# Decay rows of the first four units spread by 128-row matmuls, with more filling matmuls, in a scan and two MLP layers on one core

## Chip, core and metric

The kernel runs on one core of one Trainium2 chip. The metric is the device time of one execution in microseconds (us), taken as the median of several runs. The engines are PE (TensorE), DVE (VectorE), ACT (ScalarE), POOL (GpSimd) and SP (SyncE, which issues the DMAs).

## What is computed

A chunked linear scan with a decay feeds two MLP layers, all in float32:

```python
# scan: batch 4, 8 heads, 768 tokens, head_dim 32, state 16
L = exp(cum[i] - cum[j]) * (i >= j)          # products of the decays a
M = (C @ B.T) * L
y = M @ x + (C @ state) * exp(cum)
state = decay_full * state + sum_j B_j x_j decay_from_j
# x = y as (3072, 256)
h = x @ w_in                                  # 256 x 2048
g = where(h > 0, h, exp(min(h, 0)) - 1)
x = g @ w_out                                 # 2048 x 256
out = ((x @ w_a) * (x @ w_b)) @ w_out2        # 1536 wide
```

## The kernel before

The scan is cut into 24 units of 128 tokens of one batch with all 8 heads (`unit`, u = 0 to 23). Tokens go through the MLP in six tiles of 512 columns (phase A, `pair`), and afterwards through the gated layer (phase B, `group`). Tile 0 needs units 0 to 3, tile 1 needs units 4 to 7, and so on. The weights of w_in and w_out for tile 0 come in as raw words and are decoded on ACT, DVE and POOL (`weight`, lines 405 to 423).

**One unit.** The decay rows of its 8 heads have to stand in all 128 partitions. Units from 4 on load them by a broadcasting DMA from `a_seg` (line 522). Units 0 to 3 take them from `a32`, the first 32 rows of the decays (4 units of 8 heads), with float32 matmuls (`spread`, line 536): the weights are column r of the identity `delta`, repeated 128 times, the moving operand is `a32`, and 128 copies of row r land in PSUM. There are two groups of four heads. Then come a DVE scan against `delta` (line 560), the score matmuls of 16 rows (`cbm`, line 598, two groups of four heads, which for units 0 to 7 sit in different row ranges of `sm`), a DVE mask (line 601), the output matmuls into `ybank` (`ym`, lines 629, 633 and 637), and ACT copies of the state and of x out of `ybank` (lines 651 and 669 for units 0 to 3).

**Filling matmuls.** `warm` (line 299) multiplies a zero tile `zt` with itself in bfloat16 into the last quarter of `ybank`. Nobody reads the result. 44 of them open the program, and the planner may put more where it expects PE to be idle.

**The order.** `Plan` is a list scheduler. Each step has engines with a cost, predecessors and a due time. `emit` repeatedly takes the ready step that could start first (ties by due time) and writes it on its engine, so each engine's order is fixed before the program runs. Ahead of a PE step that starts before `FILL_TO` with over 0.2 us of expected idle time, `emit` writes fillers, their number being the idle time divided by a constant (line 140). Steps carry a `weight` for the planner's own model of PE's speed (`pe_clock`). The due times of tile 0 start at `T1`, and those of most later steps hang on it. Fillers write into `ybank`, so the first filler of a row waits for the readers of the unit before it.

Of the kernel before, what the change touches and what calls it, by code (L numbers as in the profile page):

```python
# [9 lines left out]
F32 = mybir.dt.float32  # L10
# [7 lines left out]
P = 128  # L18
NB, NH, S, D, N = 4, 8, 768, 32, 16
# [19 lines left out]
PUT_DVE = [1, 0, 1, 0, 1, 0, 1, 0, 0, 0, 0, 0, 0, 0, 0, 0, 0]  # L39
REST_DVE = [1, 1, 1, 1, 0, 1, 0, 1, 1, 0, 1, 0, 1, 0, 1, 0, 1]  # L40

T1, PAIR1, PAIR, GROUP = 22.0, 8.0, 6.2, 14.96
LEAD, GAP = 30.0, 11.0
NFILL, FILL_TO = 44, 30.0


class Buf:
# [10 lines left out]
class Plan:  # L58
# [11 lines left out]
    def add(self, engines, fn, *after, due, port=False, pad=0.0, weight=1.0, nb=0.7):  # L70
        flat = []
        for a in after:
            flat += a if isinstance(a, list) else [a]
        self.steps.append((engines, fn, [a for a in flat if a is not None], due, port, pad, weight, nb))
        return len(self.steps) - 1
# [14 lines left out]
    def emit(self, go=True):  # L90
        n = len(self.steps)
        self.work = {}
        left, then, ends = [0] * n, [[] for _ in range(n)], [None] * n
        for i, s in enumerate(self.steps):
            for a in set(s[2]):
                left[i] += 1
                then[a].append(i)
        free = dict.fromkeys(("PE", "ACT", "DVE", "POOL", "SP"), 0.7)
        port, dma, done = 0.0, 0.0, 0
        self.log = []  # L100
        ready = []

        def enter(i):
            engines, fn, after, due, prt, pad, weight, nb = self.steps[i]
            opts = []
            for e, c in engines.items():
                at = nb
                for a in after:
                    end, ea = ends[a]
                    end += (self.SYNC[ea] if ea != e else self.SAME[e]) + (pad if ea != e else 0.0)  # L110
                    if end > at:
                        at = end
                opts.append((e, c, at))
            ready.append((due, i, opts, prt))

        for i in range(n):
            if not left[i]:
                enter(i)
        while ready:
            best = None  # L120
            for k, (due, i, opts, prt) in enumerate(ready):
                end = None
                for e1, c1, at in opts:
                    s1 = free[e1] if free[e1] > at else at
                    if e1 == "POOL" or (e1 == "DVE" and prt):
                        if port > s1:
                            s1 = port
                    if e1 == "SP":
                        e, start, c = e1, s1, c1
                        break  # L130
                    if end is None or s1 + c1 < end:
                        e, start, end, c = e1, s1, s1 + c1, c1
                key = (math.floor(start / self.WIN), due, i)
                if best is None or key < best[0]:
                    best = key, k, i, e, start, c
            _, k, i, e, start, c = best
            due, _, _, prt = ready.pop(k)
            if e == "PE":
                if self.fill and go and start < FILL_TO and start - free["PE"] > 0.2:
                    m = int((start - free["PE"]) / 0.06)  # L140
                    self.fill(m)
                    self.pe_clock(free["PE"], 0.055 * m, 1.0)
                end = self.pe_clock(start, c, self.steps[i][6])
                free[e] = end
            elif e == "SP":
                end = start
                for kb in c:
                    dma = max(dma, end + 1.75) + kb / 250.0
                    end += 0.45
                free[e], end = end, dma + 0.6  # L150
            else:
                end = start + c
                free[e] = end
                if e == "POOL" or prt:
                    port = end
            if go:
                self.steps[i][1](e)
            self.log.append((i, e, start, end))
            ends[i] = end, e
            done += 1  # L160
            for t in then[i]:
                left[t] -= 1
                if not left[t]:
                    enter(t)
        assert done == n
        return max(free.values())
# [3 lines left out]
def kernel(  # L170
# [14 lines left out]
    nc = tc.nc  # L185
# [4 lines left out]
    def tl(shape, dt, name):  # L190
        return sb.tile(shape, dt, name=name, tag=name)


    delta = tl([P, 4, P], F32, "delta")
# [70 lines left out]
    def flat4(bf):  # L265
        return bf.ap.rearrange("p h i -> p (h i)") if len(bf.ap.shape) == 3 else bf.ap
# [5 lines left out]
    add = plan.add  # L272
# [4 lines left out]
    def nxt(ring, name):  # L277
        k = cnt.get(name, 0)
        cnt[name] = k + 1
        return ring[k % len(ring)]  # L280
# [42 lines left out]
                                     op0=ALU.mult, op1=ALU.add)  # L323


    a32 = tl([4 * NH, P], F32, "a32")

    def decay_0(e):
        nc.vector.tensor_scalar(a32, a32, 1.0, 1e-6, op0=ALU.min, op1=ALU.max)
        nc.vector.memset(a32[:, 0:1], 0.0)  # L330

    d0 = -40.0
    i_a0 = add({"SP": [16]}, lambda e: nc.sync.dma_start(a32, al[0:4 * NH, :]), due=d0 - 1)
    i_dec0 = add({"DVE": 0.3}, decay_0, i_a0, due=d0 - 1)
    i_z = add({"POOL": 0.2}, zeros, due=d0)
    i_warm = add({"PE": 0.055 * NFILL}, lambda e: warm(NFILL), i_z, due=d0)
# [2 lines left out]
    i_ones = add({"POOL": 1.6}, ones, due=d0)  # L339
# [146 lines left out]
    def unit(u, due):  # L486

        c, b = divmod(u, NB)
        s, r = divmod(u, NG)
# [7 lines left out]
        pd = 0.6 if u >= UPT else 0.0  # L497
# [26 lines left out]
        if n:  # L524
            i_ab = add({"SP": [512]}, ld_a, ab.take(), i_seg, due=due - ld, nb=due - ld - 10)
        else:

            sp, cb_ = ([accb[0], accb[1]], [nxt(cb1, "cb1") for _ in range(2)]) if u < 2 else (
                [nxt(rest3, "r3") for _ in range(2)], [nxt(rest3, "r3") for _ in range(2)])
            i_ab = []  # L530
            ab_old = ab.take()
            for g in range(2):
                def spread(e, g=g):
                    for h in range(4):
                        r = u * NH + 4 * g + h
                        nc.tensor.matmul(flat4(sp[g])[:, h * P:(h + 1) * P], delta[0:4 * NH, 0, r:r + 1].to_broadcast([4 * NH, P]),
                                         a32, start=True, stop=True)

                i_ab.append(add({"PE": 1.08}, spread, sp[g].take(), i_dec0, i_ones, ab_old, due=due - 1))
                sp[g].users.append(i_ab[-1])  # L540
        if s:
            i_sm = add({"SP": [512]}, ld_sm, sm.take(), i_parts[s], due=due - ld, nb=due - ld - 10)
            smu = sm
        else:
            if u % 2 == 0:
                first_sm[0] = sb_.take()
            i_sm = add({"SP": [64, 64]}, ld0, first_sm[0], due=due - ld, nb=due - ld - 10)
# [37 lines left out]
        for g in range(2):  # L585
            h4 = slice(4 * g, 4 * g + 4)

            cb = cb_[g] if n == 0 else cbb

            def cbm(e, g=g, cbank=cb.ap if len(cb.ap.shape) == 3 else cb.ap.rearrange("p (h i) -> p h i", h=4)):  # L590
                for h in range(4):
                    if s == 0:
                        q = slice(h * P, (h + 1) * P)
                        t = sm32[row + 32 * g:row + 32 * g + N]
                    else:
                        q = slice((4 * g + h) * P, (4 * g + h + 1) * P)
                        t = sm.ap
                    nc.tensor.matmul(cbank[:, h, :], t[:, 0, q], t[:, 1, q], start=True, stop=True)  # L598

            def mask(e, h4=h4, cbank=cb.ap if len(cb.ap.shape) == 3 else cb.ap.rearrange("p (h i) -> p h i", h=4)):  # L600
                nc.vector.tensor_mul(lt[:, h4], cbank, lt[:, h4])

            i_cb = add({"PE": 0.28 if s else 1.0}, cbm, cb.take(), i_sm, due=due, pad=pd)
            smu.users.append(i_cb)
            i_k = add({"DVE": 0.685}, mask, i_cb, i_scan[g], i_le, due=due)
            cb.users += [i_cb, i_k]
            i_msk.append(i_k)
# [749 lines left out]
```

## Time and profile before

| | before |
|---|---|
| median of 3 runs | 637.32 us (636.58 to 639.22) |
| the profiled execution | 636.4 us |
| its span in the trace | 634.7 us |
| PE busy | 625.9 us, 99% of the span, 3540 matmuls |
| DVE, ACT, POOL busy | 61%, 59%, 54% |

The engines' busy time is an average over stages. A PE that is busy without a gap may still run at half of its speed, so its granted clock is read beside its busy time. The chain of waits is followed back from the last instruction; where it names PE, PE was what the end waited for.

### The profile page before, as it was taken

The numbers are of one execution on the slowest core, as the hardware profiler recorded it, in microseconds if no ns is written. First come the engines' busy times: TensorE is split into PE (matmuls) and PEld (weight loads), VectorE is DVE, ScalarE is ACT, GpSimd is POOL, SyncE is SP. The second block draws the span as 40 slices with busy tenths as digits, with TensorE's granted clock in tenths as the row PEclk, the third lists the DMA queues.
The fourth block names the chain that finished last, engine by engine and source line by source line (L and its number), as shares of the span: only waits on it lengthen the run. The fifth ranks groups of instructions, "written<-read, shape, count | busy, mean of one in ns | idle before, by whom it ended". The sixth has DMA issues, their size and how long they took to land.

```text
span 634.7 us, 9280 instructions
## 1 busy us (share of the span) xinstructions
PE 625.9 (99%) x3540; PEld 490.2 (77%) x3540; DVE 386.8 (61%) x517; ACT 375.5 (59%) x536; POOL 340.3 (54%) x260
## 2 busy tenths in 40 slices
PE   9999999999999999999999999999999999999996
PEld 8875545778877788777888888888888888888885
DVE  6558886888755976987654565545633447333333
ACT  2237667657776786666677755456554456654553
POOL 2034347354765566556448287567755566555552
PEclk8579999999999999999999999999999999999999
DMA  7926643666759755620000000000100000100001
GB/s 243 322 86 220 229 142 99 226 239 195 228 161 311 237 173 158 208 84 0 2 1 0 2 0 1 0 2 0 67 2 0 1 1 1 67 1 0 1 0 67
DMA packets 33308, 59.89 MB, mean 94 GB/s; under 512 B 2736, under 2 KB 13808, under 8 KB 33264
## 3 DMA queue, kind: packets, MB, share of 16 engines
q1 hardware_dynamic: 33264, 59.30, 28.5%
q8 instruction: 28, 0.46, 0.3%
q14 instruction: 16, 0.13, 0.1%
HBM read 47.56 MB, written 11.73 MB: 93 GB/s over the span
## 4 chain that ended last, share of the span: by engine, by line
PE 90%; DMA 3%; DVE 2%; POOL 2%; issue 1%; ACT 1%; DVEq 0%; ACTq 0%; SPq 0%; POOLq 0%
PE up L1036 5%; PE up L1033 5%; PE up L1032 5%; PE up L695 5%; PE up L704 5%; PE up L705 5%; PE up L707 5%; PE acc L720 5%; PE acc L716 4%; PE acc L717 4%; PE acc L695 4%; PE acc L1104 4%; PE acc L1105 4%; PE acc L1106 4%; PE cbank L598 3%; PE cbank L1104 3%
## 5 line engine op out<-in xcount | busy, mean ns | idle before, releaser
L1133 DVE TENSOR_TENSOR x<-x 128x512 f32<-128x512 f32 x36 | 29.9, 835 | 82.0 <-POOL x L1177 81.6
L1139 POOL TENSOR_TENSOR gl<-x,gh 128x512 fp32r<-128x512 f32 x35 | 48.8, 1394 | 38.2 <-ACT gh L1136 36.0
L802 ACT ACTIVATE e<-up 128x1024 f32<-128x1024 f32 x44 | 45.2, 1027 | 31.5 <-PE up L707 26.0
L1177 POOL TENSOR_TENSOR x<-e,x 128x512 f32<-128x512 f32 x36 | 46.2, 1303 | 32.3 <-ACT e L1116 26.5
L716 PE MATMUL acc<-gh,hi_w_out 128*128 128x512 f32 x160 | 63.4, 396 | 0.0
L823 POOL TENSOR_TENSOR gl<-e,gh 128x1024 fp32r<-128x1024 f32 x20 | 50.4, 2521 | 22.6 <-ACT gh L816 20.0
L717 PE MATMUL acc<-gh,lo_w_out 128*128 128x512 f32 x160 | 62.3, 390 | 0.0
L806 ACT ACTIVATE e<-e,bias 128x1024 f32<-128x1024 f32 x44 | 50.8, 1154 | 1.0
L720 PE MATMUL acc<-gl,hi_w_out 128*128 128x512 f32 x160 | 51.1, 395 | 0.0
L560 DVE TENSOR_TENSOR_SCAN ab<-ab,delta 128x512 f32<-128x512 f32 x36 | 50.7, 1429 | 0.0
L812 DVE SCALAR_TENSOR_TENSOR up<-e,up 128x512 f32<-128x512 f32 x40 | 27.7, 693 | 24.1 <-ACT e L806 23.3
L1124 DVE TENSOR_TENSOR p<-acc,p 128x512 f32<-128x512 f32 x36 | 24.5, 688 | 28.5 <-PE acc L1106 26.7
L704 PE MATMUL up<-xh,hi_w_in 128*128 128x512 f32 x96 | 39.5, 411 | 1.5 <-DVE gl L821 0.8
L1139 POOL TENSOR_TENSOR gl<-p,gh 128x512 fp32r<-128x512 f32 x18 | 23.8, 1323 | 31.6 <-issue 28.5
L423 POOL TENSOR_TENSOR m<-m,raw 128x1024 int32<-128x1024 int32 x10 | 25.1, 2512 | 25.6 <-DVE m L413 19.1
L705 PE MATMUL up<-xh,lo_w_in 128*128 128x512 f32 x96 | 37.6, 392 | 0.6 <-DVE lo_w_in L367 0.6
L1033 PE MATMUL up<-gh,lo_w_out 128*128 128x512 f32 x96 | 37.5, 391 | 0.0
L1032 PE MATMUL up<-gh,hi_w_out 128*128 128x512 f32 x96 | 37.4, 390 | 0.0
L716 PEld LDWEIGHTS acc<-gh,hi_w_out 128*128 128x128 f32 x160 | 30.0, 188 | 7.2 <-issue 1.0
L717 PEld LDWEIGHTS acc<-gh,lo_w_out 128*128 128x128 f32 x160 | 30.1, 188 | 5.9
L720 PEld LDWEIGHTS acc<-gl,hi_w_out 128*128 128x128 f32 x160 | 29.3, 188 | 5.7 <-issue 0.2
L812 DVE SCALAR_TENSOR_TENSOR e<-e,up 128x512 f32<-128x512 f32 x48 | 30.7, 680 | 4.6 <-ACT e L806 4.3
(298 smaller groups left out, 1740.0 us busy)
## 6 DMA issues: line engine op xcount, KB each, us to landing
ab<-a_seg SPq DMA_DIRECT2D x18, 512.0 KB
parts<-raw SPq DMA_DIRECT2D x64, 128.0 KB
sm<-parts SPq DMA_DIRECT2D x16, 512.0 KB
p<-in_xb SPq DMA_DIRECT2D x20, 256.0 KB
raw<-in_w_out SPq DMA_DIRECT2D x4, 1024.0 KB
fx<-in_w_out SPq DMA_DIRECT2D x3, 1024.0 KB
out_t<-m SPq DMA_DIRECT2D x12, 256.0 KB
raw<-in_w_in SPq DMA_DIRECT2D x2, 1024.0 KB
```

The costliest lines, as they stand in the source:

```text
L560: nc.vector.tensor_tensor_scan(lt[:, h4].rearrange(flat), lt[:, h4].rearrange(flat) if n else flat4(sp[g]), delta.rearrange(flat), 0.0, op ...
L695: nc.tensor.matmul(ps, w_mm(name, wm, f, c), src, start=start, stop=stop)
L704: nc.tensor.matmul(ps, w_mm(name, whi, f, c), xh[:, c, :], start=(c == 0), stop=False)
L705: nc.tensor.matmul(ps, w_mm(name, wlo, f, c), xh[:, c, :], start=False, stop=False)
L716: nc.tensor.matmul(accs[m], w_mm(name, whi, f, m), gh, start=(f == 0), stop=False)
L717: nc.tensor.matmul(accs[m], w_mm(name, wlo, f, m), gh, start=False, stop=False)
L720: nc.tensor.matmul(accs[m], w_mm(name, whi, f, m), gl, start=False, stop=(f == last))
L806: nc.scalar.activation(gf, gf, AF.Identity, bias=bias[:, 0:1])
L812: nc.vector.scalar_tensor_tensor(u[:, k, :] if on_dve else gf[:, k, :], gf[:, k, :], 0.0, u[:, k, :], op0=ALU.min, op1=ALU.max)
L1032: nc.tensor.matmul(a4[m].ap, w_mm("w_out2", whi, f, m), gh, start=first, stop=False)
L1033: nc.tensor.matmul(a4[m].ap, w_mm("w_out2", wlo, f, m), gh, start=False, stop=False)
L1139: eng[e].tensor_sub(tap("l" + w), tap(wa), tap("h" + w).bitcast(F32))
```

## The change

Two things change in the first stage, and the planner's numbers with them. `a32` gets 128 rows instead of 32 (64 KB instead of 16 KB by DMA), and `spread` multiplies all 128 rows, with a column of the identity of 128 rows: the result is the same, since the identity picks one row. Fillers may be written up to 50 instead of 30 us of planned time, and a little denser. The planner's costs of `spread` and `cbm` go down, `cbm` of 16 rows gets a low weight, and `T1` moves from 22 to 25.

```diff
-T1, PAIR1, PAIR, GROUP = 22.0, 8.0, 6.2, 14.96
+T1, PAIR1, PAIR, GROUP = 25.0, 8.0, 6.2, 14.96
-NFILL, FILL_TO = 44, 30.0
+NFILL, FILL_TO = 44, 50.0
@@ emit
-                    m = int((start - free["PE"]) / 0.06)
+                    m = int((start - free["PE"]) / 0.054)
@@ tile_scan_mlp_kernel
-    a32 = tl([4 * NH, P], F32, "a32")
+    a32 = tl([P, P], F32, "a32")
-    i_a0 = add({"SP": [16]}, lambda e: nc.sync.dma_start(a32, al[0:4 * NH, :]), due=d0 - 1)
+    i_a0 = add({"SP": [64]}, lambda e: nc.sync.dma_start(a32, al[0:P, :]), due=d0 - 1)
@@ unit
-                        nc.tensor.matmul(flat4(sp[g])[:, h * P:(h + 1) * P], delta[0:4 * NH, 0, r:r + 1].to_broadcast([4 * NH, P]),
+                        nc.tensor.matmul(flat4(sp[g])[:, h * P:(h + 1) * P], delta[:, 0, r:r + 1].to_broadcast([P, P]),
                                          a32, start=True, stop=True)
-                i_ab.append(add({"PE": 1.08}, spread, sp[g].take(), i_dec0, i_ones, ab_old, due=due - 1))
+                i_ab.append(add({"PE": 0.9}, spread, sp[g].take(), i_dec0, i_ones, ab_old, due=due - 1))
-            i_cb = add({"PE": 0.28 if s else 1.0}, cbm, cb.take(), i_sm, due=due, pad=pd)
+            i_cb = add({"PE": 0.28 if s else 0.9}, cbm, cb.take(), i_sm, due=due, pad=pd, weight=1.0 if s else 0.125)
```

The new numbers move steps on every engine. After the 49 opening fillers the old PE order has two more rows of fillers, of 11 and of 4; the new one has five, of 28, 7, 18, 18 and 15.

The first place is PE from the spread of unit 2 on (`acc_117` and `acc_118` take the spread, `p_75` belongs to unit 1, `sm_77` holds the scores' operands of units 2 and 3). Before:

```order
L536 MATMUL acc_117<-a_120,delta 128x128 x4
L633 MATMUL ybank<-ab_79,p_75 32x128 x8
L637 MATMUL ybank<-xe,p_75 32x64 x4
L536 MATMUL acc_118<-a_120,delta 128x128 x4
L598 MATMUL cbank<-sm_77 128x128 x4
L598 MATMUL acc_117<-sm_77 128x128 x4
L299 LDWEIGHTS zt
L299 MATMUL ybank<-zt 128x128
```

And now:

```order
L536 MATMUL acc_117<-a_120,delta 128x128 x4
L536 MATMUL acc_118<-a_120,delta 128x128 x4
L598 MATMUL cbank<-sm_77 128x128 x4
L633 MATMUL ybank<-ab_79,p_75 32x128 x8
L637 MATMUL ybank<-xe,p_75 32x64 x4
L299 LDWEIGHTS zt
L299 MATMUL ybank<-zt 128x128
```

Both spread groups of unit 2 now stand together, the two score groups of unit 2 are parted, and the fillers (28 of them, then the second score group) stand directly behind the output matmuls of unit 1, whose bank they write.

The second place is PE around the output of unit 3 (`f_lo_w_out_98` and `f_lo_w_out_100` hold its operands, `up_115` and `up_116` the first MLP matmuls of tile 0). Before:

```order
L695 MATMUL up_115<-x_93,m_102 128x256 x2
L695 MATMUL up_116<-x_93,m_102 128x256 x4
L633 MATMUL ybank<-f_lo_w_out_98,f_lo_w_out_100 32x128 x8
L637 MATMUL ybank<-xe,f_lo_w_out_100 32x64 x4
L598 MATMUL cbank<-sm_76 128x128 x4
```

And now:

```order
L598 MATMUL cbank<-sm_76 128x128 x4
L633 MATMUL ybank<-f_lo_w_out_98,f_lo_w_out_100 32x128 x8
L637 MATMUL ybank<-xe,f_lo_w_out_100 32x64 x4
L299 LDWEIGHTS zt
L299 MATMUL ybank<-zt 128x128
```

The score group of unit 4 moves ahead of the output of unit 3, the MLP matmuls of the first half-tile are done earlier, and 18 fillers follow the output of unit 3, again behind the readers of `ybank`.

## Rows read from the trace of the kernel before

**Rows 1.** The page: PE's share, and PE's granted clock in 40 slices.

```profile
PE 625.9 (99%) x3540; PEld 490.2 (77%) x3540; DVE 386.8 (61%) x517; ACT 375.5 (59%) x536; POOL 340.3 (54%) x260
...

```

**Rows 2.** Stretches of PE: from:to, sum, busy (matmuls), granted clock, DMA share, GB/s.

```profile
10.00:11.00 1.00, 1.00 (x28) 1.00 1.08 231
11.00:11.50 0.50, 0.50 (x14) 0.79 0.99 352
...
38.50:39.00 0.50, 0.50 (x24) 0.90 1.03 426
```

**Rows 3.** PE matmuls by line and shape, 11.3 to 38.5 us: count, busy, mean.

```profile
L695 PE MATMUL up<-x,m 128*128 128x256 f32 x16 | 7.5, 650 | 0.0
L536 PE MATMUL acc<-a,delta 32*128 32x128 f32 x24 | 6.2, 436 | 0.0
L598 PE MATMUL acc<-sm 16*128 16x128 f32 x24 | 5.2, 436 | 0.0
L598 PE MATMUL up<-sm 16*128 16x128 f32 x16 | 3.0, 427 | 0.0
L536 PE MATMUL cbank<-a,delta 32*128 32x128 f32 x8 | 2.1, 436 | 0.0
...
L598 PE MATMUL cbank<-sm 16*128 16x128 f32 x8 | 1.9, 416 | 0.0
```

**Rows 4.** Chain of waits at the low clock: start us, us on the chain, what.

```profile
16.31 2.00 PE acc L536 x8
...
21.04 1.29 PE ybank L299 x11
...
28.68 1.01 PE ybank L633 x16
...
29.90 3.02 PE acc L598 x16
32.92 5.42 PE up L695 x12
```

**Rows 5.** The same chain before and after the low clock.

```profile
1.06 4.51 PE ybank L299 x49
5.57 1.98 PE acc L536 x16
7.55 0.56 PE cbank L598 x5
...
8.66 0.11 PE acc L536
...
9.00 1.45 PE acc L536 x13
10.44 0.62 PE ybank L633 x16
11.07 0.11 PE ybank L637 x8
...
39.16 1.08 PE cbank L598 x8
40.24 2.79 PE up L695 x12
...
51.87 5.15 PE up L695 x12
```

**Rows 6.** Order of time on ACT: the copies out of ybank of unit 0.

```profile
11.37 0.36 ACT L669 COPY x<-ybank 128x256 f32<-128x256 f32 x1
```

**Rows 7.** Order of time on DVE: a32, a mask, a weight.

```profile
2.61 0.21 DVE L329 TENSOR_SCALAR a<-a 32x128 f32<-32x128 f32 x1 [0.51 <-DMA a<-in_al]
...
40.35 0.69 DVE L601 TENSOR_TENSOR f_hi_w_out<-cbank,f_hi_w_out 128x512 f32<-128x512 f32 x1 [3.05 <-PE cbank L598]
...
49.82 1.61 DVE L423 CUSTOM_DVE_ANT_0 m<-fx,m 128x2048 uint16<-128x2048 uint16 x1
```

## The prediction

> **What bounds the kernel now.** I read the page first. PE is busy for 99% of the span, but the row of its granted clock has a hole in the first slices [rows 1]. Stretches of PE show where: the clock falls inside 11.0 to 11.5 us and is back inside 38.5 to 39.0 [rows 2]. With a mean of 0.79 over 11.0 to 11.5 the fall is at about 11.3, and with 0.90 over the later half microsecond the rise is at about 38.6: some 27.3 us at 0.50, the lower of the two levels (1.2 instead of 2.4 GHz). PE was busy without a gap all the while, before the fall too [rows 2]. What stood on it then tells more: in the microseconds before the fall it ran spreads of 32 rows, scores of 16 rows and outputs of 32 columns, and it rose at the end of twelve whole-array matmuls in a row, 32.92 to 38.34 [rows 4, 5]. The chain of waits runs on PE through all of this without a break, so here a microsecond of PE is a microsecond of the end. DVE confirms it from the other side: it waits 3.05 us for PE's scores of unit 4 [rows 7].
>
> **What a full clock would save.** The stretch from 11.3 to 38.5 us holds 32 spread instructions, 48 score instructions and 16 first-layer ones [rows 3], beside outputs and 15 fillers (11 of them in rows 4). Each kind also ran at the other clock:
> - Spreads: 2.00/8 = 0.250 us against 1.98/16 = 0.124 [rows 4, 5]. 32 x 0.126 = 4.0.
> - Scores: 3.02/16 = 0.189 at the low clock [rows 4]. At the full one the sixteen of unit 0 went through from 7.55 to 9.00, 0.091 each, since their two groups overlapped, and a lone group takes 1.08/8 = 0.135 [rows 5]. The new order keeps two of three units paired and parts unit 2: 32 x 0.098 + 16 x 0.054 = 4.0 (2.6 if all ran alone, 4.7 if all paired).
> - First layer: 5.42/12 = 0.452 against 2.79/12 = 0.233 [rows 4, 5]. 16 x 0.219 = 3.5.
> - Outputs of units 1 and 2: 2 x (1.01 - 0.62) = 0.8 [rows 4, 5].
>
> The sum is 12.3 us. A plain count agrees: half of 27.3 is 13.7, and the scores do not halve.
>
> **What the change costs, if the clock holds.**
> - A spread of 128 rows: no row shows it. A whole-array float32 instruction with 256 columns takes 0.233, so 0.116 for 128 columns, which is below the 0.124 of the 32-row one [rows 5]. Bounds: 0.116 to 0.124 each, that is -0.3 to 0 over 32. I take 0.
> - Lost overlap: spreads of 32 rows went through beside scores in other rows. Of the sixteen spread instructions of unit 1 three were through by 9.00, 13 were left, and the first stands at 8.66, ahead of the last scores [rows 5]. With 128 rows there is no row left for a neighbour. Three at each of two places, 0.11 each: 0.7 (bounds 0.3, for one place, and 1.8, if all eight instructions of a group had passed at both).
> - Fillers: 86 behind the opening ones, 15 before. At the low clock one takes 1.29/11 = 0.117 [rows 4], so half, 0.059, at the full one. 86 x 0.059 - 15 x 0.117 = +3.3. An end from the other side: the opening 49 take 4.51 us [rows 5], 0.092 each, partly at the low clock: that would make it +6.1. I take 3.3. They are fixed in number, so where PE is already late they are not free.
> - Waits that the fillers bring: two rows of fillers stand directly behind an output, and the first filler waits until ACT has read the bank. For unit 0 PE's output ended at 11.18 and ACT's copy ran to 11.73 [rows 5, 6]; with a hand-over as long as the one from PE to ACT there, 0.19, PE stands for 0.75 at each: 1.5. The row of 15 waits in the same way for the readers of unit 4, with other matmuls between: 0 to 1, I take 0.5. Behind the waiting fillers stand the second scores of unit 2 and the first-layer matmuls, so this is on the path.
> - a32 of 64 KB: its DMA must land before DVE's clamp, which started at 2.61 [rows 7], and the spread starts at 5.57 behind the opening fillers [rows 5]. Nearly 3 us of cover; 48 KB more cost nothing. If that cover went, it would cost what the landing is late.
> - The moved DMAs on SP (a load of x and of decay rows ahead of a weight's words): covered as long as the weight still comes before its use, which is the third rival.
>
> Together: -12.3 + 3.3 + 2.0 + 0.7 = -6.3 us. The profiled execution took 636.4 us, span 634.7 plus 1.7 around it, so it would take 630.1. The median of before, 637.3, lies 0.9 above that execution; from the median I get 631.0. From about 47 us to the end PE carries the chain with hardly a gap, so what it gains early should stay. With the scores' and waits' ends this case spans -8.0 to -4.0: 629.3 to 633.3.
>
> **Rival 1: the clock drops again for a part (634.8).** For it: around the two fillers behind outputs PE now stands for 0.75 us, and between them run 16-row scores and 32-column outputs, the kind that stood ahead of the old fall. Against it: 128-row spreads and fillers now stand before and after. A drop at the first place makes 28 fillers 28 x 0.059 = 1.6 dearer. One at the second place meets 18 fillers (1.1), some eight first-layer instructions (1.8) and unit 4's scores (0.9, both groups): 3.8 with little to end it soon. The first costs 1.6, both 5.4: the gain of 6.3 shrinks to between 4.7 and 0.9. I take 2.5 left.
>
> **Rival 2: the clock stays low as before, slower (645).** The change then does not do what it must. At 0.117 each, 86 fillers cost 10.1 instead of 1.8: +8.3; the bank waits stay, +2.0, and the lost overlap is some 1.1 at the low clock (three at 0.11, three at 0.25). That is +11.4 or 648.7 at the worst; if the clock comes back in the densest filler rows, half: about 643 to 645. It decides whenever less than about half of the old low stretch is lifted (6.0 of 12.3 is what the fillers, waits and lost overlap take).
>
> The Trainium skill, page "TensorE: Matmul & The Clock Gate", section "What's actually happening", says that the clock follows how busy PE has been recently. By that alone this rival would come true, since PE was already busy without a gap and only rows are added. The trace does not agree with it read so: busy for the whole of 10 to 11.5 us, the clock fell. The page also advises to put small matmuls in separate row groups so that they run at once (section "Why this matters for your kernels"), which speaks against 128 rows; by it the lost overlap would be at its upper end, 1.8, and the sum -5.2 instead of -6.3.
>
> **Rival 3: PE is early, and another engine is late (634.5).** DVE finished the third weight at 51.43 [rows 7], and PE started on it at 51.87 [rows 5]: a margin of 0.44 us. If DVE cannot come forward with PE, 3 to 4 us go there. Against it: DVE's time before was spent waiting for PE (3.05 us at one mask alone [rows 7]), so its chain moves forward too. Later waits on DVE, POOL and the DMAs between 110 and 215 us are reshuffled by the new order; I allow 1.5 us to both sides.
>
> **How the numbers follow.** Clock held: 0.50, 631.0. Dropped for a part: 0.25, 634.8. Low for most of the time: 0.14, 645. Other engines late: 0.11, 634.5. A measurement of this kernel can tell about 0.5% from no change, that is 634.1 and 640.5. Below 634.1 lie nearly all of the first case, four tenths of the second and of the third: 0.64. Between lie 0.14 of the second, 0.06 of the third and a little of the first and the slow one: 0.22. Above lies 0.14. The range leaves out the slow case and the best end of the first: 627.5 to 638.5.
>
> **What would show it.** Right: a granted clock of 1.00 from 12 to 38 us, spreads at 0.124 in unit 2 and 3, the fillers behind units 1 and 3 released by ACT's copy of x after some 0.75 us, unit 4's output on PE about 6 us earlier, and PE full from there on. Rival 1: one or two short stretches at 0.50 between 15 and 45 us. Rival 2: the hole in the clock as long as before. Rival 3: a full clock, but idle time of PE before the third weight or between 45 and 115 us. The prediction would be wrong in its sign if the fillers ran at the low clock, and wrong in size above all if the scores keep less of their overlap.

## The result and the profile after

The changed kernel takes 629.72 us in the median of 4 runs (629.16 to 630.62); the kernel before took 637.36 (636.58 to 639.22) beside it. The ratio is 0.9877, with a 95% interval of 0.9852 to 0.9903. It is faster by 1.2%, 7.6 us, where 6.3 us and 631.0 were forecast. Medians, ranges and ratios, here and below, leave out runs over 1.5% above the fastest of their kernel: one of e1's (650.3 us) and two of e3's (643.5 and 644.0 us).

PE's granted clock in 40 slices on the page of the kernel before, beside [rows 1]:

```profile
PEclk8579999999999999999999999999999999999999
```

The page of the changed kernel, PE's share and its granted clock:

```profile
PE 619.1 (99%) x3611; PEld 486.7 (77%) x3611; DVE 394.7 (63%) x519; ACT 374.2 (60%) x536; POOL 339.4 (54%) x258
...
PEclk9999999999999999999999999999999999999999
```

PE's busy time fell by 6.8 us although 71 more matmuls ran, and the hole in the clock is gone. Stretches of PE of the changed kernel (from:to, sum, busy (matmuls), granted clock, DMA share, GB/s), where [rows 2] showed a fall to 0.50:

```profile
15.00:20.00 5.00, 4.39 (x67) 1.00 1.02 353
...
30.00:35.00 5.00, 4.39 (x70) 1.00 0.91 250
```

The clock is 1.00 in every stretch from 10 to 40 us. In these two PE stands for 0.61 us each, behind the outputs of units 1 and 3, and fillers wait there. The chain of waits of the changed kernel (start us, us, what), against [rows 4] and [rows 5]:

```profile
1.06 5.41 PE ybank L299 x49
...
8.51 0.75 PE cbank L598 x5
...
10.15 1.98 PE acc L536 x16
...
18.09 0.16 PE ybank L637 x8
...
18.27 0.21 ACT state L651
18.48 0.28 ACT x L669
...
18.81 1.72 PE ybank L299 x28
...
21.61 0.50 PE ybank L299 x7
...
29.93 1.00 PE ybank L299 x18
...
33.30 1.16 PE ybank L299 x18
...
41.66 0.84 PE ybank L299 x15
```

Spreads of 128 rows take 1.98/16 = 0.124 us, as those of 32 rows did at the full clock [rows 5]. The five rows of fillers take 1.72 + 0.50 + 1.00 + 1.16 + 0.84 = 5.2 us. After unit 1 the chain leaves PE for the two ACT copies out of the bank and returns to the first filler.

One more number is needed to compare the runs below. In the order of time on PE I take the start of the first spread and the start of unit 4's output (line 629). The distance between the two, the **stage**, leaves out the opening fillers, whose time differs from one execution to the next (4.42 to 5.41 us for the same 49). It still holds the first sixteen spreads, which took 2.00 to 3.78 us in the traces, as the clock was up sooner or later. Before the change, in the order of time on PE:

```profile
5.50 2.05 PE L536 MATMUL acc<-a,delta 32*128 32x128 f32 x16
...
45.10 0.43 PE L629 MATMUL ybank<-p,sbd 128*32 128x128 f32 x8
```

And after it:

```profile
6.26 2.25 PE L536 MATMUL acc<-a,delta 128*128 128x128 f32 x16
...
38.33 0.43 PE L629 MATMUL ybank<-p,sbd 128*32 128x128 f32 x8
```

The stage went from 39.6 to 32.1 us. (In the new order four first-layer instructions, 1.06 us, come behind the stage's end that came ahead of it before.)

### The profile page after: what moved, and what is told of

Read it like the earlier page. It is cut to its first block, busy times and chain, and to the rows that moved or that the text cites. A ratio compares the mean times of both kernels' runs of the same rounds, so it can differ in the third digit from the quotient of the medians.

```text
span 628.4 us, 9413 instructions
## 1 busy us (share of the span) xinstructions
PE 619.1 (99%) x3611; PEld 486.7 (77%) x3611; DVE 394.7 (63%) x519; ACT 374.2 (60%) x536; POOL 339.4 (54%) x258
## 4 chain that ended last, share of the span: by engine, by line
PE 96%; DMA 1%; DVE 1%; ACT 1%; issue 0%; SPq 0%; DVEq 0%; ACTq 0%; POOL 0%; POOLq 0%
PE up L704 6%; PE acc L720 6%; PE acc L716 6%; PE up L705 6%; PE acc L717 5%; PE up L707 5%; PE up L1036 5%; PE up L1033 5%; PE up L1032 5%; PE up L695 5%; PE acc L695 4%; PE acc L1105 4%; PE acc L1104 4%; PE acc L1106 4%; PE cbank L598 3%; PE ybank L1105 3%
## 5 line engine op out<-in xcount | busy, mean ns | idle before, releaser
L812 DVE SCALAR_TENSOR_TENSOR up<-e,up 128x512 f32<-128x512 f32 x40 | 27.7, 693 | 15.6 <-ACT e L806 14.8
L601 DVE TENSOR_TENSOR ab<-cbank,ab 128x512 f32<-128x512 f32 x37 | 25.4, 686 | 15.7 <-PE cbank L598 9.2
L717 PEld LDWEIGHTS acc<-gh,lo_w_out 128*128 128x128 f32 x160 | 30.1, 188 | 5.9
L716 PEld LDWEIGHTS acc<-gh,hi_w_out 128*128 128x128 f32 x160 | 30.1, 188 | 5.9
```

The source lines that it names most:

```text
L716: nc.tensor.matmul(accs[m], w_mm(name, whi, f, m), gh, start=(f == 0), stop=False)
L717: nc.tensor.matmul(accs[m], w_mm(name, wlo, f, m), gh, start=False, stop=False)
L812: nc.vector.scalar_tensor_tensor(u[:, k, :] if on_dve else gf[:, k, :], gf[:, k, :], 0.0, u[:, k, :], op0=ALU.min, op1=ALU.max)
```

## The experiments

Theory: the depth of the spreads holds the clock. Rivals: the fillers hold it, since PE only has to be kept from standing still; or the new order brought the gain. All kernels of one order write the same instructions in the same sequence but for what the edit names. "Later fillers" are those behind the opening row; leaving them out also takes five of the 49 opening ones.

| kernel | order | rows | later fillers | median us (range, runs) | ratio to before (95%) | stage us |
|---|---|---|---|---|---|---|
| before | old | 32 | 15 | 636.8 (634.3 to 638.9, 19) | 1 | 39.6 |
| changed | new | 128 | 86 | 629.7 (629.2 to 630.6, 4) | 0.9877 (0.9852 to 0.9903) | 32.1 |
| e1 | new | 32 | 86 | 640.0 (637.1 to 641.9, 9) | 1.0047 (1.0023 to 1.0070) | 38.6 |
| e2 | new | 128 | 0 | 625.0 (623.9 to 629.9, 4) | 0.9835 (0.9783 to 0.9886) | 27.7 |
| e3 | new | 32 | 0 | 634.8 (630.5 to 637.5, 8) | 0.9969 (0.9937 to 1.0000) | 38.0 |
| e4 | old | 128 | 15 | 623.3 (622.8 to 624.7, 4) | 0.9797 (0.9760 to 0.9833) | 27.9 |
| e5 | old | 128 | 0 | 624.3 (623.5 to 625.3, 4) | 0.9807 (0.9775 to 0.9839) | 29.8 |
| e6 | old | 64 | 15 | 636.6 (632.7 to 640.2, 10) | 1.0000 (0.9972 to 1.0028) | 37.8 |
| e7 | old | 96 | 15 | 623.3 (623.1 to 624.4, 4) | 0.9793 (0.9767 to 0.9820) | 27.9 |
| e8 | old | 128 | 15, opening 20 | 622.1 (621.8 to 623.4, 4) | 0.9776 (0.9749 to 0.9803) | 29.5 |
| e9 | new | 128 | 42 | 627.3 (626.8 to 629.0, 4) | 0.9876 (0.9851 to 0.9902) | 30.1 |
| e10 | old | 128 | 15, opening 8 | 622.9 (622.2 to 629.7, 4) | 0.9822 (0.9769 to 0.9876) | 36.9 |
| e11 | old | 128 | 15, opening 20 | 622.0 (621.5 to 622.9, 4) | 0.9785 (0.9766 to 0.9805) | 29.3 |

The stage is that of the one profiled execution of each. Each ratio is to the runs of the kernel before that were timed beside it: their median was 637.4 us for the changed kernel, 636.8 for e1 to e8 and 635.4 for e9 to e11.

### Depth undone (e1), fillers undone (e2), both (e3), depth alone (e4)

e1 is the changed kernel with

```diff
-    a32 = tl([P, P], F32, "a32")
+    a32 = tl([4 * NH, P], F32, "a32")
-delta[:, 0, r:r + 1].to_broadcast([P, P])
+delta[0:4 * NH, 0, r:r + 1].to_broadcast([4 * NH, P])
```

and the DMA of a32 as before the change.

> The changed kernel, its order and its 86 fillers kept, but the decay rows spread by matmuls of 32 rows again. Theory (the depth of the spread holds the clock): the clock falls at 11 to 13 us, as before the change, and comes back behind the row of 28 fillers at about 22 us; PE's spreads of units 2 and the scores run at the low clock, and the time is 632 to 637 us. Rival (PE only has to be kept busy, fillers alone do it): granted clock 1.00 throughout and the time of the changed kernel, 629 to 631 us.

Stretches of PE of e1:

```profile
9.50:10.00 0.50, 0.50 (x9) 0.82 1.07 369
10.00:26.00 16.00, 15.39 (x129) 0.50 0.98 293
...
26.50:27.00 0.50, 0.50 (x4) 0.61 0.90 169
```

With the same order and the same fillers, 32 rows lose the clock from about 9.8 to 26.9 us. The rise comes amid the scores behind the row of 28 fillers, some 12 us sooner than before the change, but the 28 fillers took 3.14 us at the low clock, against 1.72 in the changed kernel: e1 is slower than the kernel before by 0.5%. I had expected 632 to 637 us. In this order the depth is decisive, and fillers without it cost more than they bring.

e2 is the changed kernel with the fillers left out and the planner's accounts kept:

```diff
-                    self.fill(m)
+                    pass
```

> The changed kernel, order kept, without the 86 fillers behind the opening ones; the spreads keep 128 rows. If the depth alone holds the clock: it stays at 1.00, the fillers' 5.2 us and the waits of 0.6 us twice go from PE's path as far as PE does not have to wait there for data, 624 to 629 us. If the fillers are needed too: the clock falls between 15 and 22 us, the scores and first-layer matmuls up to about 38 us run at half speed, 632 to 638 us.

Its chain of waits, second half of the stage:

```profile
28.67 0.16 PE ybank L637 x8
...
28.85 0.21 ACT state L651
29.06 0.28 ACT x L669
...
29.39 1.13 PE up L695 x4
```

The clock is 1.00 without a later filler in the profiled execution. By their times (623.9 to 625.4 us) it held in three runs of four, and the median of 625.0 us is 4.7 below the changed kernel; the stage is 4.4 shorter. Because of the fourth run the intervals of the two ratios overlap. The first-layer matmuls now wait for ACT's copy themselves at the second place, 0.6 us, so that wait was not the fillers' alone. The fourth run took 629.9 us with a mean granted clock of 0.987 over the run, against 0.998 and more in the other three: there the clock was lost for a part, and without a trace of that run it stays open where. That is my first rival, in the kernel without fillers.

e3 joins both edits.

> The new order and planner numbers alone: spreads of 32 rows, no fillers behind the opening ones. Both theories: the clock falls at about 11 to 13 us and is back at 36 to 45 us, 634 to 640 us, within 0.5% of before. If the new order itself brought the gain (a rival to both): 629 to 632 us.

The order of time on PE in e3:

```profile
5.86 3.78 PE L536 MATMUL acc<-a,delta 32*128 32x128 f32 x16
...
31.83 1.13 PE L695 MATMUL up<-x,m 128*128 128x256 f32 x4
```

Here 44 opening fillers did not bring the clock up in the profiled execution: 16 spread instructions take 3.78 us, twice the 1.98 of [rows 5], and the full rate of the first layer, 1.13 for four, stands only at 31.83. (The record of the clock shows 1.00 ahead of its first change, and the mean of this execution is 0.999. A high mean alone therefore does not say that the clock held; the durations and the times do.) The runs scatter from 630.5 to 637.5 us, and the interval of the ratio ends at 1.0000: the new order alone brought nothing that can be told from no change.

e4 is the kernel before with spreads of 128 rows and nothing else.

> The kernel before, its order and its 15 fillers kept, with spreads of 128 rows alone. If depth alone holds the clock: 1.00 through the first 45 us and 626 to 631 us. If the fillers are needed too: the clock falls later than before, at 15 to 22 us (the stretch of outputs and scores of units 1 and 2), and the time is 632 to 637 us.

Its chain of waits:

```profile
15.40 1.09 PE acc L536 x8
...
18.12 0.72 PE ybank L299 x11
18.84 0.95 PE acc L536 x8
19.79 0.22 PE ybank L299 x4
...
24.15 2.79 PE up L695 x12
```

All of it runs at the full clock. 623.3 us is better than the 626 to 631 that I had expected, and the interval of its ratio lies below that of the changed kernel. So the depth of the spread alone gives more than the whole gain, and what the change adds beside it takes some of it back.

### Without the old fillers (e5), and how deep a spread must be (e6, e7)

e5 is e4 with the fillers left out, as in e2.

> The order before the change with spreads of 128 rows, and without its 15 fillers behind the opening ones. If the depth of the spreads alone holds the clock: 1.00 throughout, and the 15 fillers' 0.9 us go from PE's path, 622 to 624 us. If the fillers were what kept it up in the run before: a drop between 18 and 25 us, where they stood, and 624 to 629 us.

Stretches of PE of e5:

```profile
15.00:20.00 5.00, 4.56 (x58) 1.00 1.04 393
20.00:20.50 0.50, 0.45 (x3) 0.63 0.90 266
20.50:23.50 3.00, 3.00 (x11) 0.50 1.05 275
```

PE stands for 0.44 us ahead of unit 3's spread, where the 11 fillers were, and the clock drops some 1.2 us later, for some 3.4 us. The stage is 1.9 us longer than that of e4, 0.4 of it in the first sixteen spreads (2.37 us against 2.00), and the median is 1.0 us higher, though the ranges of the two overlap. By these two executions the 15 fillers earn more than the 0.9 us (0.72 + 0.22, the 11 and the 4) that they take; the times do not decide it. As far as the trace goes, depth alone did not hold the clock through this wait.

e6 and e7 are e4 with 64 and 96 rows in place of 128.

> The order and the 15 fillers before the change, spreads of 64 rows. If the clock follows how much of the array works: it holds less surely than with 128 rows, a drop at 11 to 15 us in part of the runs, 624 to 635 us and a wide spread. If any depth over 32 rows were enough: 623 to 624 us, as with 128 rows. If only the full array counts: the time of before, 635 to 638 us.

> The order and the 15 fillers before the change, spreads of 96 rows. The second score group of unit 1 stands in rows 96 to 111, which the spread then leaves free: if the overlap of scores with the spread is worth what I priced (0.3 to 0.5 us at one place), it comes back there, and with a clock that holds the time is 622.5 to 624 us. If 96 rows do not hold the clock: 625 to 636 us.

Stretches of PE of e6:

```profile
15.50:16.00 0.50, 0.50 (x17) 0.80 0.97 377
16.00:36.00 20.00, 20.00 (x107) 0.50 0.96 289
36.00:36.50 0.50, 0.50 (x3) 0.72 1.06 135
```

With 64 rows the clock falls at 15.8 us, some 4.5 us later than with 32, and stays low for some 20 us: no gain in the median. With 96 rows it holds, and the time is that of 128. So of the four depths, 32 and 64 take the time of before, 96 and 128 that of e4; no depth between 64 and 96 was run. Sixteen spreads take 1.98 us at the full clock with 64 rows as with 96, and PE has the same instructions in the same order in e6 and e7. What I had expected to come back with 96 rows did not: PE's chain in e7 has

```profile
11.62 1.64 PE up L598 x16
13.26 1.09 PE acc L536 x8
```

with unit 1's sixteen scores alone for 1.64 us, as with 128 rows, although their second group stands in rows 96 to 111. In e6, where both groups (rows 64 to 79 and 96 to 111) are clear of the spread's 64 rows, it is the same:

```profile
12.37 1.64 PE up L598 x16
14.01 1.08 PE acc L536 x8
```

So it is not by keeping scores and spreads apart that a deep spread holds the clock: they ran apart in e6 too, and its clock fell.

### Half of the fillers (e9), and a shorter opening (e8, e10, e11)

e9 is the changed kernel with `self.fill(m // 2)`.

> The changed kernel and its order with half of each row of fillers behind the opening ones (14, 3, 9, 9, 7). Without any, three runs of four kept the clock and one lost part of it, at 625.0 us in the median. If fillers cost their own time on PE: half of the 4.7 us comes back, 627 to 628 us with a clock that holds. If PE would have waited there anyway: 629 to 630 us, as with all of them. If half of them leave holes that matter: over 630 us and a clock below 0.99.

By the medians 2.4 us of the 4.7 come back, by the stage 2.0 of 4.4, and no run took more than 629.0 us. By the ratio it stands where the changed kernel stands, because the kernel before ran at 635.4 us beside it and at 637.4 beside the other. The kernel before scatters with its clock, and these two do not, so I go by the stage; on the ratios alone this one is not decided.

e8 is e4 with 20 opening fillers, e10 with 8, and e11 is e8 once more.

```diff
-lambda e: warm(NFILL)
+lambda e: warm(20)
```

> The order before the change with spreads of 128 rows and 20 opening fillers instead of 44 (the five that follow them stay). If the spreads raise the clock as the fillers did: they start at about 3.5 instead of 5.7 us, run at the low clock in part, and the time is that with 44 fillers or up to 1 us less, 622 to 624 us. If the opening row is needed: the clock stays low for some microseconds longer, 624 to 630 us.

> The order before the change with spreads of 128 rows and 8 opening fillers instead of 44 (20 gave 622.1 us). If the spreads raise the clock themselves: they start near 3.1 us, when the decay rows have landed, run the first 3 to 4 us at the low clock, and the chain is carried by the first weight's DMA as with 20: 622 to 623 us. If the opening row is what raises it: the clock comes later by several us, and the time is 624 to 628 us.

> The same program as the one with 20 opening fillers (spreads of 128 rows, order and 15 later fillers of before), timed once more beside the others: 621.5 to 623 us, below both the kernel before and the changed one, and a granted clock of 1.00 from the first rise on. A median above 624 us would say that its lead over 44 opening fillers (623.3) was chance.

With 20 the first spread starts at 3.70 us, and both times the median is 622 us, some 1.2 below e4. The traces show less of it: unit 4's output starts at 33.24 us in e8 and 33.03 in e11, against 33.57 in e4. With 8 three runs took 622.2 to 623.3, but the profiled one took 629.7. Its order of time on PE:

```profile
3.34 3.75 PE L536 MATMUL acc<-a,delta 128*128 128x128 f32 x16 [0.71 <-DVE a L330]
...
21.23 1.97 PE L536 MATMUL acc<-a,delta 128*128 128x128 f32 x8
...
25.40 1.11 PE L536 MATMUL acc<-a,delta 128*128 128x128 f32 x8
```

PE waits 0.71 us for the decay rows, and everything runs at the low clock until about 23 us, where the eight spreads of 1.97 us end. In e4 spreads of 128 rows held a clock that was up; in this execution they did not soon bring it up behind a short opening. e8 and e11, with the ratio 0.978, have the lowest medians found; the intervals of their ratios overlap that of e4.

## Why the prediction was right, step by step

**The bound.** Right. The low clock on a PE that never stood still was what bounded the first stage, and lifting it moved the end.

**What a full clock saves: 12.3 us.** Right in size. e4 has the full clock, with the overlap lost in it: its stage is 39.6 - 27.9 = 11.7 us shorter, some 0.8 of it in the 15 old fillers, which stand in another term of the sum. Paired scores were priced somewhat low, at 0.091 us each; they take 1.64/16 = 0.103. Behind the stage another 2.2 us went (span less the start of unit 4's output: 589.6 before, 621.0 - 33.57 = 587.4 in e4), 1.4 of it waits of PE on DVE, which sum to 3.3 us in the kernel before and to 1.9 in e4. I had allowed 1.5 us to both sides there.

**128 rows cost no time.** Right: 0.124 us each.

**Lost overlap: 0.7 us for two places.** Too small, and its cause is open. Unit 0's scores and unit 1's spread took 7.55 to 10.45, 2.90 us, in [rows 5] and take 8.51 to 12.13, 3.62 us, now: 0.7 at the first place alone. The second, unit 1's scores and the first spread group of unit 2, ran at the low clock before. PE's chain of the kernel before:

```profile
11.18 2.24 PE up L598 x13
...
14.06 1.02 PE acc L536 x5
```

And that of e4:

```profile
11.99 1.64 PE up L598 x16
13.62 1.09 PE acc L536 x8
```

Half of the 3.91 us that this took before (11.18 to 15.09) is 1.95, against 2.72 in e4 (11.99 to 14.71): some 0.8 by this estimate, so 1.5 for both places, within the bounds of 0.3 to 1.8. Missing free rows, the reason that the prediction gave, are not the whole of it: with 64 and with 96 rows unit 1's scores did not overlap with the spread either. The advice on separate row groups (the Trainium skill, page "TensorE: Matmul & The Clock Gate", section "Why this matters for your kernels") is about slices of 32 rows. The trace of the kernel before agrees, as far as three of the sixteen spreads of 32 rows went through beside scores; spreads of 64 or 96 rows are not what it speaks of.

**Fillers: 5.1 us gross.** Right, 5.2.

**Waits behind the readers of the bank: 2.0 us.** Somewhat too large: 0.60 at each of the two places, and nothing at the third. e2 shows that one of the two is there without fillers.

**a32 and its DMA: nothing.** Right. In the order of time on DVE of the changed kernel, against [rows 7]:

```profile
2.62 0.23 DVE L329 TENSOR_SCALAR a<-a 128x128 f32<-128x128 f32 x1 [0.52 <-DMA a<-in_al]
```

**The sum.** The terms gave -6.3 us and the profiled spans differ by 634.7 - 628.4 = 6.3. That they agree so closely is luck. The lost overlap was some 0.8 dearer, and the waits were 0.8 cheaper. The first spread started 0.76 us later, because the opening fillers took 5.41 instead of 4.51 us. Behind the stage the work got 1.4 us shorter: that part of the span went from 589.6 to 590.1 us, though 1.06 us of first-layer instructions and 0.84 us of fillers are new in it. Half of that, 0.7, is PE standing for 1.8 instead of 2.5 us between the stage and 400 us. The medians differ by 7.6.

**Rival 1** (the clock drops again for a part) is not seen in the changed kernel: its profiled execution has a clock of 1.00 from 10 us on, and its four runs lie within 1.5 us. A drop as short as that of e5 might not show in the times of the other three. It does come in e2's fourth run and in e5. **Rival 2** (it stays low, slower) is what e1 shows: without the depth the same kernel is slower than before. I had priced the slow side at up to +11.4 us; it was +3.2; the low stretch ended early, behind the row of 28 fillers. The reading of the Trainium skill, page "TensorE: Matmul & The Clock Gate", section "What's actually happening", by busy time alone predicted that rows would not matter; e4 against before, and e6 against e7, differ in rows alone and disagree with it. **Rival 3** (another engine is late) did not come: PE's longest waits in the changed kernel are these (line, waited for, us, times, longest), and none stands at the third weight:

```profile
PE cbank L598 <- DVE ab L601: 1.4, 1, 1.4
PE ybank L299 <- ACT x L669: 1.2, 2, 0.6
PE ybank L299 <- POOL zt L295: 1.1, 1, 1.1
PE up L1036 <- DVE gl L1139: 0.9, 1, 0.9
```

What the prediction did not ask is whether the two halves of the change need each other. By the medians, in the new order depth is worth 10.3 us with fillers (e1 against the changed kernel) and 9.8 without (e3 against e2), while fillers cost 5.2 us with 32 rows and 4.7 with 128. e3's runs lie up to 7 us apart, so these differences show no need of one half for the other. The one sign of a use of the new fillers is that no run of the changed kernel stands out, where without them one of four lost the clock for a part; four runs each do not decide it.

## What to carry to other kernels

Read the granted clock beside PE's busy time: here a PE that was 99% busy ran at half its speed for some 27 us, from a stretch of matmuls of 16 and 32 rows on. The 96 more rows of a spread took no time (0.124 us either way), while the 86 fillers took 5.2 us. Try the two halves of such a change apart, since here the depth alone gave 13.5 us and the rest of the change took back about 6. Where an order is written by a planner, measure a stage in the trace from a fixed start to a fixed end, so that most of the scatter of the opening does not hide what the edit does.

## What the runs showed of the hardware that I had not expected

- The clock held with spreads of 96 and 128 rows and fell with 64 (at 15.8 us) and 32 (at 11.3 us), with the same order, the same fillers and a PE that was busy throughout (e7, e4, e6, the kernel before). All rows loaded hold real decays; whether rows count by being used or by what stands in them was not run.
- The same 49 opening fillers took between 4.42 us (e7) and 5.41 us (the changed kernel), and in e3 44 of them did not bring the clock up in the profiled execution, where the low clock lasted until past 30 us. The scatter of e3's runs, 1.1%, may come from that; no run shows it.
- 0.44 us of standing, amid scores of 16 rows and outputs of 32 columns, was followed by a drop of the clock for 3.4 us (e5), while the changed kernel stood twice for 0.6 us with fillers directly behind and kept it. That the fillers made the difference is not shown: e2 stood for 0.6 us as well, with first-layer instructions behind, and kept it.
- Float32 scores of 16 rows overlapped with spreads of 32 rows, but not with spreads of 64 rows, which left both groups of unit 1 free (e6), or of 96 rows, which left one of them free (e7); why is open.
